# Attention and an expert layer on one core: the kv products of two heads as separate half-width matmuls, left-over tiles whole

## The chip, the cores and the metric

One core of a Trainium2 chip runs the program. The metric is the device time of one execution in microseconds. Before the change three runs took 923.88, 923.95 and 925.03 us; their median is 923.95 us. The engines named below are PE (matrix engine, with PEld for the loads of its stationary operand), DVE (vector), ACT (scalar), POOL and SP, whose queue issues most of the DMAs.

## The reference

```python
def _attn_ref(q, k, v):                    # each (8, 8, 576, 64): batch, head, row, column
    q_s = np.exp(q - np.max(q, axis=-1, keepdims=True))
    q_s = q_s / (np.sum(q_s, axis=-1, keepdims=True) + 1e-09)
    k_s = np.exp(k - np.max(k, axis=2, keepdims=True))
    k_s = k_s / (np.sum(k_s, axis=2, keepdims=True) + 1e-09)
    kv = np.einsum('bhsd,bhse->bhde', k_s, v)
    return np.einsum('bhsd,bhde->bhse', q_s, kv)

def _moe_ref(x, w_in, w_out, s, b):        # x (4608, 512), w_in (512, 2048), w_out (2048, 512)
    r = np.maximum(x @ w_in, 0.0)
    return (s * (r * r) + b) @ w_out
```

The attention's result, heads beside each other, is x. q is made a softmax along its 64 columns, k along its 576 rows; kv is a 64x64 matrix for each head. All arrays are f32.

## The kernel before

**Tiling.** The two heads 2u and 2u+1 form a unit u, two units a pair pr of four heads. A batch has two pairs, 16 in all. The 576 rows of a head are four tiles of 128 rows and a left-over of 64 (`NQ` 4, `LEFT` 64, `NT` 5). A unit's k tile is 128 partitions by five tiles by two heads by 64 columns.

**Expert layer.** For each block of 512 rows and each of 16 chunks of w_in and w_out, twelve h matmuls (line 524) make a 128x512 tile, ACT and DVE turn it into g, and twelve acc matmuls (line 597) add it to the output. h and acc use operands split in a high and a low part, so three products each. There are nine blocks: one for each batch, and one for the left-over rows of all.

**Batch 0** (lines 292 to 389) runs beside the loading and splitting of the weights (`conv_w`, lines 181 to 219). Its streams, `k_stream`, `kv_stream`, `q_stream`, the weight conversions and the steps of the expert layer, are put in one order for PE, DVE, ACT and SP by a planner (`Order`), which works with an estimated cost and a due time for each piece: `Op("PE", 2.6, ...)` is the kv group. `k_stream` transposes a unit's k tile by tile (line 300), takes the maximum and the exponential along the free axis and transposes back (lines 313 and 314). v lies head by head (`by_head`), 64 columns each.

**Later batches** go through `pair` (line 391 on), a generator that is advanced between the steps of the expert layer; a scheduler then fixes the order of each engine. There v lies by tile with both heads of a unit beside each other and a 129th column of ones (`v_tile`), which gives the sum of k's exponentials in the same matmul. The rows beyond the left-over are zeros in k, set by a memset after each exponential (line 425).

**The kv product**, in both places: for each unit and row tile one matmul with both heads' 128 k columns as the stationary operand and both heads' v as the moving one.

```python
nc.tensor.matmul(kv[:, i, :], kts[i][:, n].rearrange("p h d -> p (h d)"), vt[:, i, n, :], start=(n == 0), stop=(n == NT - 1))   # line 444
```

Of the 128x128 result only the two 64x64 blocks on the diagonal, head with its own head, are used (lines 341 and 453); the other two mix two heads and are dropped. In batch 0 the product and the transposes of the left-over tile take only its 64 rows (`m = P if n < NQ else LEFT`, lines 299 and 327). After the product come DVE's `z` and reciprocal, the scaling of four 64x64 blocks into `kvf`, its split, and the product with q (`xp`).

Of the kernel before, what the change touches and what calls it, by code (L numbers as in the profile page):

```python
# [8 lines left out]
F32 = mybir.dt.float32  # L9
# [3 lines left out]
AF = mybir.ActivationFunctionType  # L13
ALU = mybir.AluOpType
# [11 lines left out]
def attention_moe(ctx: ExitStack, tc: tile.TileContext, q, k, v, w_in, w_out, s, b, out):  # L26
    nc = tc.nc
    B, H, S, D = q.shape
    DM, FF = w_in.shape
    DO = w_out.shape[1]  # L30
    P = 128
    NP = H // 2
    NFC = FF // P
    NQ = 4
    LEFT = S - NQ * P
    NT = NQ + 1
# [17 lines left out]
    ps = ctx.enter_context(tc.tile_pool(name="ps", bufs=1, space=bass.MemoryType.PSUM))  # L54


    ident = const.tile([P, P], F32, name="ident")
    make_identity(nc, ident)

    kvfs = [const.tile([P, 2, 2, D], F32, name=f"kvf{i}") for i in range(2)]  # L60
    for t in kvfs:
# [4 lines left out]

    KQ, VW = 4 * NT * D, 2 * NT * (2 * D + 1)
    second = xpool.tile([P, 2 * NP * TB], F32, name="raw1", tag="x")  # L70
    raws = [
        (const.tile([P, KQ], F32, name="k0"), const.tile([P, KQ], F32, name="q0"), const.tile([P, VW], F32, name="v0")),
        (second[:, 0:KQ], second[:, KQ:2 * KQ], second[:, 2 * KQ:2 * KQ + VW]),
    ]

    def by_head(t):
        return t[:, 0:KQ].rearrange("p (h n d) -> p h n d", h=4, d=D)

    def by_tile(t):
        return t.rearrange("p (u n h d) -> p u n h d", u=2, h=2, d=D)  # L80

    def v_tile(t):
        return t.rearrange("p (u n e) -> p u n e", u=2, n=NT)

    for kt, qt, vt in raws:
        nc.gpsimd.memset(by_head(qt)[LEFT:P, :, NQ, :], 0.0)
    nc.gpsimd.memset(by_tile(raws[0][0])[LEFT:P, :, NQ], 0.0)

# [150 lines left out]
    def sources(pr):  # L241
        bb, hq = divmod(pr, NP // 2)
        h0 = 4 * hq

        def main(t, i, n):
            return t[bb, h0 + i:h0 + i + n, 0:NQ * P, :].rearrange("h (p n) d -> p h n d", n=NQ)

        def left(t, i, n):
            return t[bb, h0 + i:h0 + i + n, NQ * P:S, :].rearrange("h p d -> p h d")

        return main, left

    def load_k(pr, i):
        main, left = sources(pr)
        kt = by_tile(tiles[pr][0])
        for h in range(2):
            nc.sync.dma_start(kt[:, i, 0:NQ, h], main(k, 2 * i + h, 1)[:, 0])
        nc.sync.dma_start(kt[0:LEFT, i, NQ], left(k, 2 * i, 2))

    def load_heads(pr, which, eng):  # L260
        main, left = sources(pr)
        t = by_head(tiles[pr][which])
        eng.dma_start(t[:, :, 0:NQ, :], main((q, v)[which - 1], 0, 4))
        eng.dma_start(t[0:LEFT, :, NQ, :], left((q, v)[which - 1], 0, 4))

    def loads(pr):
        tiles[pr] = raws[0]
        main, left = sources(pr)
        for i in range(2):
            load_k(pr, i)  # L270
        load_heads(pr, 1, nc.sync)
        vt = v_tile(tiles[pr][2])
        if pr == NP:
            nc.gpsimd.memset(vt[LEFT:P, :, NQ, 0:2 * D], 0.0)
            nc.gpsimd.memset(vt[:, :, :, 2 * D:2 * D + 1], 1.0)
        for i in range(2):
            for h in range(2):
                nc.sync.dma_start(vt[:, i, 0:NQ, h * D:(h + 1) * D], main(v, 2 * i + h, 1)[:, 0])
            nc.sync.dma_start(vt[0:LEFT, i, NQ, 0:2 * D].rearrange("p (h d) -> p h d", h=2), left(v, 2 * i, 2))

    def bc(t, shape):
        return t.unsqueeze(3).to_broadcast(shape)

# [2 lines left out]
    def wide(u):  # L288

        return ("acc", 2) if u < NP else ("big", 1)  # L290

    def k_stream(u):
        pr, i = divmod(u, 2)
        due, (tag, bufs) = DUE[u], wide(u)
        yield Op("PE", 0.6, due, needs=[f"k{u} there"], take=[tag, "ke"])
        kt = by_tile(tiles[pr][0])
        kT = ps.tile([P, 2, 512], F32, name=f"kT_{u}", tag=tag, bufs=bufs).rearrange("p a b -> p (a b)")
        for n in range(NT):
            m = P if n < NQ else LEFT
            nc.tensor.transpose(kT[:, n * P:n * P + m], kt[0:m, i, n].rearrange("p h d -> p (h d)"), ident[0:m, 0:m])  # L300
        yield Op("DVE", 0.67, due)
        km = small.tile([P, 1], F32, name=f"km_{u}", tag="km")
        nc.vector.tensor_reduce(out=km, in_=kT[:, 0:S], axis=AX.X, op=ALU.max, negate=True)
        yield Op("ACT", 0.71, due, free=[tag])
        if pr not in zs:
            zs[pr] = small.tile([P, 2], F32, name=f"z_{pr}", tag="z")
        ke = work.tile([P, S], F32, name=f"ke_{u}", tag="qh")
        nc.scalar.activation(ke, kT[:, 0:S], AF.Exp, bias=km, accum_out=zs[pr][:, i:i + 1])

        yield Op("PE", 0.55, due, take=[tag], free=["ke"])  # L310
        kn = ps.tile([P, 2, 512], F32, name=f"kn_{u}", tag=tag, bufs=bufs).rearrange("p a b -> p (a b)")
        for n in range(NQ):
            nc.tensor.transpose(kn[:, n * P:(n + 1) * P], ke[:, n * P:(n + 1) * P], ident)
        nc.tensor.transpose(kn[0:LEFT, TB:TB + P], ke[:, TB:S], ident)
        yield Op("ACT", 0.63, due, free=[tag], gives=[f"k{u}"])
        nc.scalar.copy(kt[:, i, 0:NQ], kn[:, 0:TB].rearrange("p (n h d) -> p n h d", n=NQ, h=2))
        nc.scalar.copy(kt[0:LEFT, i, NQ], kn[0:LEFT, TB:TB + P].rearrange("p (h d) -> p h d", h=2))

    def kv_stream(pr):
        us = (2 * pr, 2 * pr + 1)  # L320
        due = DUE[us[1]]
        yield Op("PE", 2.6, due, needs=[f"k{u}" for u in us] + [f"v{pr} there"], take=["sm"], gives=[f"kv{pr}"])
        kt, vt = by_tile(tiles[pr][0]), by_head(tiles[pr][2])
        kv = ps.tile([P, 512], F32, name=f"kv_{pr}", tag="sm", bufs=1)[:, 0:4 * D].rearrange("p (u e) -> p u e", u=2)
        for i in range(2):
            for n in range(NT):
                m = P if n < NQ else LEFT
                nc.tensor.matmul(
                    kv[:, i].rearrange("p (h d) -> p h d", h=2), kt[0:m, i, n].rearrange("p h d -> p (h d)"),
                    vt[0:m, 2 * i:2 * i + 2, n, :], start=(n == 0), stop=(n == NT - 1)  # L330
                )
        yield Op("DVE", 0.15, due)
        z = zs.pop(pr)
        nc.vector.tensor_scalar(z, z, 1e-9, None, op0=ALU.add)
        zr = small.tile([P, 2], F32, name=f"zr_{pr}", tag="zr")
        nc.vector.reciprocal(zr, z)
        yield Op("ACT", 1.28, due, free=["sm"], gives=[f"kvf{pr}"])
        for i in range(2):
            for h in range(2):
                r = slice(h * D, (h + 1) * D)  # L340
                nc.scalar.activation(kvfs[pr % 2][r, i, h, :], kv[r, i, r], AF.Copy, scale=zr[r, i:i + 1])

    def q_stream(u):
        pr, i = divmod(u, 2)
# [46 lines left out]
    def pair(pr):  # L391
        us = (2 * pr, 2 * pr + 1)
        bb = us[0] // NP
        kt, qt, vt = tiles.pop(pr)
        kt, qt, vt = by_tile(kt), by_head(qt), v_tile(vt)
        kts, qts = [kt[:, i] for i in range(2)], [qt[:, 2 * i:2 * i + 2] for i in range(2)]

        def sm(n):
            return ps.tile([P, 512], F32, name=f"{n}_{pr}", tag="sm", bufs=1)
# [9 lines left out]
        kT = sm("kT")  # L409
# [19 lines left out]
        for i in range(2):  # L429
            u, qt = us[i], qts[i]  # L430
# [6 lines left out]
            qes.append(qe)  # L437
            yield

        EW = 2 * D + 1  # L440
        kv = sm("kv")[:, 0:2 * EW].rearrange("p (u e) -> p u e", u=2)
        for i in range(2):
            for n in range(NT):
                nc.tensor.matmul(kv[:, i, :], kts[i][:, n].rearrange("p h d -> p (h d)"), vt[:, i, n, :], start=(n == 0), stop=(n == NT - 1))  # L444
        z = small.tile([P, 2], F32, name=f"z_{pr}", tag="z")
        nc.vector.tensor_scalar(z, kv[:, :, 2 * D], 1e-9, None, op0=ALU.add)
        zr = small.tile([P, 2], F32, name=f"zr_{pr}", tag="zr")
        nc.vector.reciprocal(zr, z)
        kvf = kvfs[pr % 2]
        for i in range(2):  # L450
            for h in range(2):
                r = slice(h * D, (h + 1) * D)
                nc.vector.tensor_scalar(kvf[r, i, h, :], kv[r, i, r], zr[r, i:i + 1], None, op0=ALU.mult)
        kvhl = work.tile([P, 2, 2, 2 * D], F32R, name=f"kvhl_{pr}", tag="m2")
        split(kvf.rearrange("p u h d -> p u (h d)"), kvhl[:, 0], kvhl[:, 1], nc.scalar.copy, nc.gpsimd)
        yield
# [38 lines left out]
        for i in range(2):  # L495
            normalize(i)
            yield
            t = transpose(i)
# [183 lines left out]
    with tc.issue_after(fetched[-1].ins):  # L682
        loads(NP)
# [67 lines left out]
```

## Time and profile before

| what | value |
|---|---|
| median of the runs | 923.95 us |
| the profiled execution, whole | 925.23 us |
| its span, first to last instruction | 923.0 us |
| mean granted clock of PE | 0.996 |
| DVE busy from 50 to 60 us | 9.90 of 10 us |
| DVE busy from 346.6 to 445 us | 48.38 of 98.4 us |
| kv groups (line 328) in batch 0 | 4, of 20 records each |
| kv groups (line 444) later | 12, of 20 records each |
| records of line 444 on PE | 240, from 172.0 to 707.9 us |

An f32 matmul appears as two records of PE and two weight loads of PEld; an f32r matmul (h, acc) as one of each. A record's shape is written rows*columns of the stationary operand, then partitions x elements of the result. Matmuls are pipelined, so their durations overlap; how long a group holds the engine is read from the chain of work or from the distance of starts.

### The profile page before, as it was taken

The page shows a single profiled execution, that of the slowest core. Times are in us where ns is not written, and L with a number is a line of the kernel's source. Part 1 is how long each engine was busy: PE and PEld are TensorE (multiplying, and loading weights), DVE is VectorE, ACT ScalarE, POOL GpSimd, SP SyncE. Part 2 cuts the span into 40 slices and gives each one's busy share as a digit, 9 for nine tenths or more (in the row PEclk, how much of TensorE's full clock was granted, in tenths as well). Part 3 has the DMA queues.
Part 4 walks back from the last instruction along what each step waited for, and adds up shares of the span by engine and source line. Part 5 has one row for each costly group of instructions (what it writes and reads, how often), then busy time and mean ns, then how long its engine had stood idle before and what let it go on. Part 6 is the DMA issues. An engine that isn't in the chain of part 4 may idle for free.

```text
span 923.0 us, 10924 instructions
## 1 busy us (share of the span) xinstructions
PE 898.4 (97%) x4240; PEld 741.0 (80%) x4240; DVE 470.8 (51%) x731; ACT 366.8 (40%) x590; POOL 82.3 (9%) x101
## 2 busy tenths in 40 slices
PE   4799999999999999999999999999999999999997
PEld 3577778888888888888888888888888888888885
DVE  5999993545364636463455445453645332223222
ACT  4899874323332333243233333232333332222222
POOL 0000000202020201110021102020202020000000
PEclk9999999999999999999999999999999999999999
DMA  8891431303031201302130313030210110001001
GB/s 224 256 376 51 140 81 46 77 4 77 4 95 30 66 16 47 78 16 68 46 77 3 77 49 78 4 78 4 85 42 0 49 46 1 1 0 46 1 1 46
DMA packets 101731, 57.33 MB, mean 62 GB/s; under 512 B 78512, under 2 KB 96944, under 8 KB 101552
## 3 DMA queue, kind: packets, MB, share of 16 engines
q1 hardware_dynamic: 99760, 54.94, 21.2%
q10 hardware_dynamic: 1920, 1.70, 0.6%
q8 instruction: 33, 0.54, 0.3%
q14 instruction: 18, 0.15, 0.1%
HBM read 46.14 MB, written 10.49 MB: 61 GB/s over the span
## 4 chain that ended last, share of the span: by engine, by line
PE 87%; DMA 4%; DVE 4%; ACT 3%; issue 1%; ACTq 0%; SPq 0%; DVEq 0%
PE acc L597 40%; PE h L524 39%; PE kv L444 3%; PE xp L487 2%; DMA st<-in_moe_w_in_dram 2%; PE qT L470 1%; DMA v<-in_v_dram 1%; DMA st<-in_moe_w_out_dram 1%; DVE low L198 1%; DVE w L214 1%; DMA raw<-in_q_dram 0%; ACT low L192 0%; ACT w L212 0%; ACT st L195 0%; DVE x L389 0%
## 5 line engine op out<-in xcount | busy, mean ns | idle before, releaser
L524 PE MATMUL h<-x,w 128*128 128x512 f32 x1728 | 425.0, 393 | 1.3 <-ACT r L557 1.2
L524 PEld LDWEIGHTS h<-x,w 128*128 128x128 f32 x1728 | 321.7, 188 | 69.3 <-ACT r L557 3.5
L597 PE MATMUL acc<-w,gh 128*128 128x512 f32 x1152 | 345.8, 393 | 1.4 <-ACT o L609 1.4
L545 DVE SCALAR_TENSOR_TENSOR r<-r,sb 128x512 f32<-128x512 f32 x128 | 101.3, 791 | 299.3 <-ACT r L544 299.2
L597 PEld LDWEIGHTS acc<-w,gh 128*128 128x128 f32 x1152 | 214.1, 188 | 45.8 <-ACT o L609 2.1
L597 PE MATMUL acc<-w,gl 128*128 128x512 f32 x576 | 211.2, 393 | 0.7 <-DVE gl L537 0.6
L544 ACT ACTIVATE r<-h 128x512 f32<-128x512 f32 x128 | 76.5, 597 | 320.4 <-PE h L524 315.7
L537 DVE SCALAR_TENSOR_TENSOR gl<-r,sb,gh 128x512 fp32r<-128x512 f32 x132 | 102.8, 778 | 75.1 <-ACT gh L546 73.0
L597 PEld LDWEIGHTS acc<-w,gl 128*128 128x128 f32 x576 | 108.2, 188 | 26.1 <-DVE gl L537 2.4
L546 ACT ACTIVATE gh<-r,sb 128x512 fp32r<-128x512 f32 x128 | 92.7, 724 | 83.7 <-DVE r L545 83.1
L434 POOL TENSOR_TENSOR q<-q,qm 128x640 f32<-128x640 f32 x24 | 30.3, 1262 | 444.6 <-DVE qm L433 444.6
L464 POOL TENSOR_TENSOR qe<-qe,qr 128x640 f32<-128x640 f32 x24 | 30.3, 1262 | 48.7 <-DVE qr L463 44.5
L444 PE MATMUL kv<-v,k 128*128 128x129 f32 x240 | 28.8, 274 | 0.0
L444 PEld LDWEIGHTS kv<-v,k 128*128 128x128 f32 x240 | 28.2, 191 | 0.5
L436 ACT ACTIVATE qe<-q 128x640 f32<-128x640 f32 x24 | 17.6, 732 | 22.7 <-POOL q L434 22.7
L424 ACT ACTIVATE k<-k 128x640 f32<-128x640 f32 x24 | 17.6, 736 | 22.3 <-DVE k L419 22.3
L460 DVE TENSOR_REDUCE qs<-qe 128x10 f32<-128x640 f32 x24 | 19.6, 818 | 12.1 <-ACT qe L436 12.0
L95 DVE TENSOR_TENSOR x<-xp,x 128x512 fp32r<-128x512 f32 x24 | 16.6, 691 | 17.8 <-ACT x L94 17.6
L487 PE MATMUL xp<-qh,kvhl 128*128 128x256 f32 (+1 forms) x96 | 23.4, 297 | 0.0
L95 DVE TENSOR_TENSOR ql<-qT,qh 128x576 fp32r<-128x576 f32 x24 | 18.2, 756 | 7.7 <-ACT qh L94 7.6
L419 DVE TENSOR_TENSOR k<-k,mb 128x640 f32<-128x640 f32 x24 | 18.6, 815 | 6.1 <-PE mb L417 6.1
L94 ACT CAST qh<-qT 128x576 fp32r<-128x576 f32 x24 | 15.4, 640 | 14.1 <-PE qT L470 14.1
(97 smaller groups left out, 569.3 us busy)
## 6 DMA issues: line engine op xcount, KB each, us to landing
st<-in_moe_w_in_dram SPq DMA_DIRECT2D x16, 512.0 KB, 9.5
st<-in_moe_w_out_dram SPq DMA_DIRECT2D x16, 512.0 KB, 9.8
out_dram<-o SPq DMA_DIRECT2D x16, 512.0 KB, 2.7
k<-in_k_dram SPq DMA_DIRECT2D x60, 128.0 KB, 3.1
q<-in_q_dram SPq DMA_DIRECT2D x14, 512.0 KB, 4.4
v<-in_v_dram SPq DMA_DIRECT2D x48, 128.0 KB, 3.0
v<-in_v_dram SPq DMA_DIRECT2D x2, 512.0 KB, 4.1
xleft<-xleft SPq DMA_DIRECT2D x16, 64.0 KB, 1.7
```

The costliest lines, as they stand in the source:

```text
L95: return eng_l.tensor_tensor(out=l, in0=src, in1=h.bitcast(F32), op=ALU.subtract)
L434: nc.gpsimd.tensor_tensor(out=qt, in0=qt, in1=bc(qm, [P, 2, NT, D]), op=ALU.subtract)
L444: nc.tensor.matmul(kv[:, i, :], kts[i][:, n].rearrange("p h d -> p (h d)"), vt[:, i, n, :], start=(n == 0), stop=(n == NT - 1))
L460: nc.vector.tensor_reduce(out=qs, in_=qe, axis=AX.X, op=ALU.add)
L464: nc.gpsimd.tensor_tensor(out=qe, in0=qe, in1=bc(qr, [P, NT, 2, D]), op=ALU.mult)
L487: nc.tensor.matmul(t[:, 0:src.stop - src.start], lhs, rhs[:, src], start=(j == 0), stop=(j == len(terms) - 1))
L524: nc.tensor.matmul(hp_, w[:, j, c, :], x[:, c, :], start=(c == 0 and i == 0), stop=(c == NP - 1 and i == 2))
L537: gls.append(nc.vector.scalar_tensor_tensor(out=gl, in0=r, scalar=b_col, in1=gh.bitcast(F32), op0=ALU.add, op1=ALU.subtract))
L544: nc.scalar.activation(r, hp_, AF.Relu)
L545: nc.vector.scalar_tensor_tensor(out=r, in0=r, scalar=s_col, in1=r, op0=ALU.mult, op1=ALU.mult)
L546: nc.scalar.activation(gh, r, AF.Identity, bias=b_col)
L597: last = nc.tensor.matmul(a, g[:, js], w_, start=(f == 0 and i == 0), stop=(f == NFC - 1 and i == 2)).ins
```

## The change

Each kv matmul of a unit becomes two, one for each head. A head's 64 k columns are the stationary operand, and its own 64 columns of v the moving one; the two heads of a unit write to the lower and the upper 64 partitions of the same PSUM columns. The products that mix two heads are no longer computed. Both places call the new function `heads`. To give each head a column of ones, v lies head by head with 65 columns in all batches (`v_tile`). The four heads' left-over rows of v come by one DMA, not two.

In batch 0 the left-over tile is used whole, so its other 64 rows in k and v of both buffers are set to zero at the start; and the planner's estimate of the kv group goes from 2.6 to 1.4.

```diff
-    KQ, VW = 4 * NT * D, 2 * NT * (2 * D + 1)
+    KQ, VW = 4 * NT * D, 4 * NT * (D + 1)
...
     def v_tile(t):
-        return t.rearrange("p (u n e) -> p u n e", u=2, n=NT)
+        return t.rearrange("p (h n e) -> p h n e", h=4, n=NT)

     for kt, qt, vt in raws:
-        nc.gpsimd.memset(by_head(qt)[LEFT:P, :, NQ, :], 0.0)
-    nc.gpsimd.memset(by_tile(raws[0][0])[LEFT:P, :, NQ], 0.0)
+        nc.gpsimd.memset(by_tile(kt)[LEFT:P, :, NQ], 0.0)
+        for t in (qt, vt):
+            nc.gpsimd.memset(by_head(t)[LEFT:P, :, NQ, :], 0.0)
...
         if pr == NP:
-            nc.gpsimd.memset(vt[LEFT:P, :, NQ, 0:2 * D], 0.0)
-            nc.gpsimd.memset(vt[:, :, :, 2 * D:2 * D + 1], 1.0)
-        for i in range(2):
-            for h in range(2):
-                nc.sync.dma_start(vt[:, i, 0:NQ, h * D:(h + 1) * D], main(v, 2 * i + h, 1)[:, 0])
-            nc.sync.dma_start(vt[0:LEFT, i, NQ, 0:2 * D].rearrange("p (h d) -> p h d", h=2), left(v, 2 * i, 2))
+            nc.gpsimd.memset(vt[LEFT:P, :, NQ, 0:D], 0.0)
+            nc.gpsimd.memset(vt[:, :, :, D:D + 1], 1.0)
+        for h in range(4):
+            nc.sync.dma_start(vt[:, h, 0:NQ, 0:D], main(v, h, 1)[:, 0])
+        nc.sync.dma_start(vt[0:LEFT, :, NQ, 0:D], left(v, 0, 4))
...
+    def heads(kv, kt, vt):
+
+        for i in range(2):
+            for n in range(NT):
+                for h in range(2):
+                    nc.tensor.matmul(
+                        kv[h * D:(h + 1) * D, i], kt[:, i, n, h], vt[:, 2 * i + h, n], start=(n == 0), stop=(n == NT - 1)
+                    )
...
         for n in range(NT):
-            m = P if n < NQ else LEFT
-            nc.tensor.transpose(kT[:, n * P:n * P + m], kt[0:m, i, n].rearrange("p h d -> p (h d)"), ident[0:m, 0:m])
+            nc.tensor.transpose(kT[:, n * P:(n + 1) * P], kt[:, i, n].rearrange("p h d -> p (h d)"), ident)
...
-        yield Op("PE", 2.6, due, needs=[f"k{u}" for u in us] + [f"v{pr} there"], take=["sm"], gives=[f"kv{pr}"])
+        yield Op("PE", 1.4, due, needs=[f"k{u}" for u in us] + [f"v{pr} there"], take=["sm"], gives=[f"kv{pr}"])
         kt, vt = by_tile(tiles[pr][0]), by_head(tiles[pr][2])
-        kv = ps.tile([P, 512], F32, name=f"kv_{pr}", tag="sm", bufs=1)[:, 0:4 * D].rearrange("p (u e) -> p u e", u=2)
-        for i in range(2):
-            for n in range(NT):
-                m = P if n < NQ else LEFT
-                nc.tensor.matmul(
-                    kv[:, i].rearrange("p (h d) -> p h d", h=2), kt[0:m, i, n].rearrange("p h d -> p (h d)"),
-                    vt[0:m, 2 * i:2 * i + 2, n, :], start=(n == 0), stop=(n == NT - 1)
-                )
+        kv = ps.tile([P, 512], F32, name=f"kv_{pr}", tag="sm", bufs=1)[:, 0:2 * D].rearrange("p (u d) -> p u d", u=2)
+        heads(kv, kt, vt)
...
-                nc.scalar.activation(kvfs[pr % 2][r, i, h, :], kv[r, i, r], AF.Copy, scale=zr[r, i:i + 1])
+                nc.scalar.activation(kvfs[pr % 2][r, i, h, :], kv[r, i], AF.Copy, scale=zr[r, i:i + 1])
...
-        EW = 2 * D + 1
-        kv = sm("kv")[:, 0:2 * EW].rearrange("p (u e) -> p u e", u=2)
-        for i in range(2):
-            for n in range(NT):
-                nc.tensor.matmul(kv[:, i, :], kts[i][:, n].rearrange("p h d -> p (h d)"), vt[:, i, n, :], start=(n == 0), stop=(n == NT - 1))
+        kv = sm("kv")[:, 0:2 * (D + 1)].rearrange("p (u e) -> p u e", u=2)
+        heads(kv, kt, vt)
...
-                nc.vector.tensor_scalar(kvf[r, i, h, :], kv[r, i, r], zr[r, i:i + 1], None, op0=ALU.mult)
+                nc.vector.tensor_scalar(kvf[r, i, h, :], kv[r, i, 0:D], zr[r, i:i + 1], None, op0=ALU.mult)
```

How the order of the instructions changes is shown at three places. The first is PE early in batch 0, at the first kv group; kT, kn and kv are the results of the transposes and the product, k, raw and v the loaded tiles. Before:

```order
L300 MATMUL kT_200<-ident,raw_88 128x128 x4
L300 MATMUL kT_200<-ident,raw_88 128x64
L328 MATMUL kv_215<-v_91,k_89 128x128 x10
L313 MATMUL kn_242<-ident,ke_228 128x128 x4
L314 MATMUL kn_242<-ident,ke_228 64x128
L300 MATMUL kT_256<-ident,raw_88 128x128 x4
L300 MATMUL kT_256<-ident,raw_88 128x64
L380 MATMUL xp_276<-qf_186,kvf_83 128x256
```

After:

```order
L308 MATMUL kT_203<-ident,raw_88 128x128 x5
L289 MATMUL kv_218<-v_91,k_89 64x64 x20
L321 MATMUL kn_251<-ident,ke_241 128x128 x4
L322 MATMUL kn_251<-ident,ke_241 64x128
L308 MATMUL kT_266<-ident,raw_88 128x128 x5
L382 MATMUL xp_283<-qf_189,kvf_83 128x256
```

The sequence is the same; the short fifth transpose is now like the other four, and ten products have become twenty.

The second place is PE at the first kv group of the later batches, between the expert layer's acc and h matmuls. Before:

```order
L597 MATMUL acc_2_1399<-w_446,gl_1424 128x512
L444 MATMUL kv_1471<-v_91,k_89 128x129 [waits DMAHW0_49,DMAHW5_49,DVE_49,DMAHW6_49,PE_49,DMAHW7_49,Activation_49,Pool_49]
L444 MATMUL kv_1471<-v_91,k_89 128x129 x3
L444 MATMUL kv_1471<-v_91,k_89 128x129 [waits DMAHW7_49,DMAHW1_49,Pool_49]
L444 MATMUL kv_1471<-v_91,k_89 128x129 [waits DMAHW2_49,DMAHW1_49,DMAHW3_49,DMAHW0_49,Activation_49]
L444 MATMUL kv_1471<-v_91,k_89 128x129 x3
L444 MATMUL kv_1471<-v_91,k_89 128x129 [waits DMAHW4_49,DMAHW2_49,Pool_49]
L524 MATMUL h_1511<-x_857,w_541 128x512 [waits Activation_49]
```

After:

```order
L596 MATMUL acc_2_1441<-w_471,gl_1466 128x512
L289 MATMUL kv_1513<-v_91,k_89 64x65 [waits DVE_49,PE_49,DMAHW5_49,Activation_49,Pool_49]
L289 MATMUL kv_1513<-v_91,k_89 64x65 [waits DMAHW6_49]
L289 MATMUL kv_1513<-v_91,k_89 64x65 x6
L289 MATMUL kv_1513<-v_91,k_89 64x65 [waits DMAHW7_49,DMAHW1_49,Pool_49]
L289 MATMUL kv_1513<-v_91,k_89 64x65
L289 MATMUL kv_1513<-v_91,k_89 64x65 [waits DMAHW7_49,DMAHW0_49,Activation_49]
L289 MATMUL kv_1513<-v_91,k_89 64x65 [waits DMAHW0_49]
L289 MATMUL kv_1513<-v_91,k_89 64x65 x6
L289 MATMUL kv_1513<-v_91,k_89 64x65 [waits DMAHW2_49,Pool_49]
L289 MATMUL kv_1513<-v_91,k_89 64x65
L523 MATMUL h_1563<-x_883,w_557 128x512 [waits Activation_49]
```

The group stands in the same surroundings, and waits for the same loads and engines, spread over more matmuls.

The third place is DVE early in batch 0, around the reciprocal of the first pair's sums z; qm and km are maxima, low and w parts of the weight conversion. Before:

```order
L352 TENSOR_REDUCE qm_236<-raw_88 128x10
L352 TENSOR_REDUCE qm_240<-raw_88 128x10
L334 TENSOR_SCALAR z_133<-z_133 128x2
L336 RECIPROCAL zr_252<-z_133 128x2
L354 TENSOR_TENSOR raw_88<-raw_88,qm_236 128x640
L303 TENSOR_REDUCE km_267<-kT_256 128x1
L354 TENSOR_TENSOR raw_88<-raw_88,qm_240 128x640
L214 TENSOR_TENSOR w_233<-low_0_166,w_233 128x512
```

After:

```order
L336 TENSOR_SCALAR z_136<-z_136 128x2
L338 RECIPROCAL zr_258<-z_136 128x2
L354 TENSOR_REDUCE qm_260<-raw_88 128x10
L354 TENSOR_REDUCE qm_272<-raw_88 128x10
L356 TENSOR_TENSOR raw_88<-raw_88,qm_260 128x640
L311 TENSOR_REDUCE km_280<-kT_266 128x1
L356 TENSOR_TENSOR raw_88<-raw_88,qm_272 128x640
L362 TENSOR_REDUCE qs_299<-qe_286 128x10
```

The reciprocal goes ahead of the two maxima of q, and the weight conversion's row moves further back.

More of the change, by code (lines that the diff above doesn't have):

```diff
@@ L438, in pair @@
             yield
-        EW = 2 * D + 1
-        kv = sm("kv")[:, 0:2 * EW].rearrange("p (u e) -> p u e", u=2)
-        for i in range(2):
-            for n in range(NT):
-                nc.tensor.matmul(kv[:, i, :], kts[i][:, n].rearrange("p h d -> p (h d)"), vt[:, i, n, :], start=(n == 0), stop=(n == NT - 1))
+        kv = sm("kv")[:, 0:2 * (D + 1)].rearrange("p (u e) -> p u e", u=2)
+        heads(kv, kt, vt)
         z = small.tile([P, 2], F32, name=f"z_{pr}", tag="z")
-        nc.vector.tensor_scalar(z, kv[:, :, 2 * D], 1e-9, None, op0=ALU.add)
+        nc.vector.tensor_scalar(z, kv[:, :, D], 1e-9, None, op0=ALU.add)
         zr = small.tile([P, 2], F32, name=f"zr_{pr}", tag="zr")
```

## The prediction

> **What bounds the kernel now.** I read the busy shares and the slices of the page first, then the chain of work that ended last, then the busy times by stage, then the kv groups themselves.
>
> ```profile
> span 923.0 us, 10924 instructions
> PE 898.4 (97%) x4240; PEld 741.0 (80%) x4240; DVE 470.8 (51%) x731; ACT 366.8 (40%) x590; POOL 82.3 (9%) x101
> ...
> PEclk9999999999999999999999999999999999999999
> ...
> PE 87%; DMA 4%; DVE 4%; ACT 3%; issue 1%; ACTq 0%; SPq 0%; DVEq 0%
> ...
> by line: PE acc L597 45.7%; PE h L524 45.2%; PE kv L444 3.5%; PE xp L487 2.5%; PE qT L470 1.7%; PE kT L411 0.3%; PE mb L417 0.3%; ACT o L609 0.2%; DVE o L609 0.1%; issue 0.0%; DVEq L609 0.0%
> ```
>
> The last of these lines is the chain asked for from 150 us to the end. There it runs on the matrix engine (PE) alone: nothing else has more than 0.2% of these 773 us, and 3.5% of them, 27 us, are the kv products of line 444. The clock is full throughout. So after 150 us a microsecond taken from PE is a microsecond off the kernel, until another engine is late; the vector engine (DVE) is busy only half of that time:
>
> ```profile
> core 0: us, PE busy (x) PEld busy (x) DVE busy (x) ACT busy (x) POOL busy (x), PEclk, DMA share, GB/s
> 80.00:90.00 10.00, 9.96 (x51) 7.63 (x50) 9.79 (x14) 9.21 (x16) 0.00 (x0) 1.00 0.11 32
> 90.00:100.00 10.00, 10.00 (x51) 8.13 (x51) 9.80 (x14) 9.15 (x14) 0.00 (x0) 1.00 0.55 141
> 100.00:110.00 10.00, 9.65 (x41) 6.76 (x39) 9.93 (x16) 9.13 (x15) 0.00 (x0) 1.00 0.69 223
> 110.00:120.00 10.00, 9.92 (x52) 7.99 (x53) 9.97 (x13) 8.93 (x16) 0.00 (x0) 1.00 0.01 2
> ...
> 150.00:248.30 98.30, 98.30 (x478) 82.47 (x477) 48.60 (x82) 34.10 (x57) 12.38 (x14) 1.00 0.19 49
> ```
>
> Batch 0 and the weights, up to 150 us, are another case: PE and DVE are both full, and a saving on PE alone is partly stopped by DVE.
>
> **The later batches, where the main term lies.** One kv group after 150 us, in the chain, and the form of its instructions:
>
> ```profile
> 170.98 1.36 PE acc L597 x6
> 172.34 2.23 PE kv L444 x20
> ...
> L444 PE MATMUL kv<-v,k 128*128 128x129 f32 x240 | 28.8, 274 | 0.0
> L444 PEld LDWEIGHTS kv<-v,k 128*128 128x128 f32 x240 | 28.2, 191 | 0.5
> ```
>
> An f32 matmul is two records, each a weight load and a pass; ten matmuls make 20 records, 2.23 us, so 0.1115 us a record. Loads of 191 ns and passes of 274 ns overlap, for one behind the other they would need far more. Twelve groups give 26.8 us, the 27 us of the chain.
>
> The change makes 20 matmuls, 40 records, of each group: 64 weight columns and 65 moving columns in place of 128 and 129. Two questions decide: what a half-size record takes, and whether the records of the two heads, which write different halves of the output's partitions, run beside each other.
>
> For the size, by proportion a record takes 0.1115 x 65/129 = 0.056 us. What 64 columns are worth elsewhere:
>
> ```profile
> L380 PE MATMUL xp<-qf,kvf 128*128 128x320 f32 x16 | 5.9, 453 | 0.0
> ...
> L380 PE MATMUL xp<-qf,kvf 128*128 128x256 f32 x16 | 5.3, 410 | 3.9 <-ACT qf L373 2.5 <-ACT kvf L341 0.7 <-DVE x L389 0.6
> ```
>
> 64 moving columns in f32 make 43 ns there, so at worst a record falls to 0.1115 - 0.043 = 0.069 us. With the heads side by side a group takes 20 x 0.056 = 1.12 to 20 x 0.069 = 1.38 us; one behind the other 2.24 to 2.76.
>
> The ends of a group have a price too if the array must empty when the width changes. In the first stage there is one such row with half the columns, a transpose between whole ones:
>
> ```profile
> 22.36 0.11 PEld L314 LDWEIGHTS kn<-ident,ke 128*64 128x64 f32 x1
> 22.46 0.47 PEld L300 LDWEIGHTS kT<-ident,raw 128*128 128x128 f32 x4
> 23.10 0.13 PEld L300 LDWEIGHTS kT<-ident,raw 64*128 64x128 f32 x1 [0.17 <-issue]
> ```
>
> The 64-column load starts 0.10 us ahead of the next whole one, with no hole, while the load with 64 rows waits 0.17 us for nothing named. Half the rows costs a hole, half the columns does not, so I put the ends at nothing, at most 0.2 us each. The Trainium skill ("TensorEngine Tiling (Array Packing)", Key Properties) says that changing the tiling mode, not just the tile, drains the engine; the hole before the 64-row load agrees, the 64-column row does not. By that rule each group would have two drains, and the saving below would be smaller by up to 12 x 0.4 = 4.8 us.
>
> That the heads run side by side no row of before shows, since each matmul there takes the whole array. The bounds are 1.12 and 2.76 us. I take 1.35, near the 1.38 of the dearer record: each matmul's own two records still follow one another, but the second of one head and the first of the other use different columns. Saved: 12 x (2.23 - 1.35) = **10.6 us**.
>
> What covers the rest here: each pair's v comes in by five DMAs and no longer six, from the sync queue, well ahead; the reciprocal and the scaling on DVE read the same 64x64 blocks; the column of ones is set once, for all later pairs. All of that lies beside PE. No wait is new: kv waits for the same loads and the same exponentials. What would be late next is the exponential's memset on POOL, and its queue is 12.4 us busy out of 98.
>
> **Batch 0.** Here the change also takes away the 64-row products and transposes, which stand between whole ones:
>
> ```profile
> 77.28 0.66 PE kn L313 x4
> ...
> 79.45 0.64 PE kT L300 x5
> 80.09 0.90 PE acc L597 x3
> ...
> 86.03 0.70 PE acc L597 x3
> ...
> 87.53 1.39 PE acc L597 x6
> 88.92 2.81 PE kv L328 x20
> 91.73 1.60 PE acc L597 x6
> ...
> 95.73 0.04 ACT x L386
> ...
> 130.08 0.69 DVE x L389
> ```
>
> A kv group takes 2.81 us, and the six acc matmuls behind it 1.60 and not 1.39: 3.02 us against 2.23 for whole tiles, so 0.8 us for four changes of height. With the halves it is 3.02 - 1.35 = 1.67 us, four times 6.7. A kT group makes the next three matmuls 0.90 and not 0.70 us: 0.2, eight times 1.6. That is 8.3 us of PE. How much shows? Between 77 and 96 us the chain runs on PE, with one kv and one kT in it: 1.67 + 0.2 = 1.9. From there to 130 us it goes through DVE and ACT, whose work doesn't change, and DVE was over 9.6 of 10 us busy. I take **1.9 us**. At best the later relief adds up too, some 5 us; at worst the order hurts: the kv estimate falls from 2.6 to 1.4 and the planner rearranges weight conversions against q work on DVE, whose longest single rows are 1.2 us. Two or three of those put ahead of something needed make +3. The three added memsets on POOL lie in the first microseconds, while k is still coming in:
>
> ```profile
> 2.50 0.31 POOL L87 MEMSET k<- 64x256 f32 x1
> ...
> L300 PE MATMUL kT<-ident,k 128*128 128x128 f32 x24 | 5.0, 347 | 8.0 <-DMA k<-in_k_dram 8.0
> ```
>
> Three more at 0.31 us end near 3.8 us; the first transpose waits for its DMA until about 8. Without that cover they would cost 0.9 us.
>
> **The sum.** 10.6 + 1.9 = 12.5 us. The profiled execution took 925.23 us (its span of 923.0 and 2.2 around it), 1.3 above the median of the runs, 923.95. 925.23 - 12.5 = 912.7, and 1.3 lower on the runs' scale: 911.4, said as **911.5**.
>
> **The rivals.**
> *The heads run one behind the other.* For it: nothing in before has two matmuls in different columns, and the loads could have one path, in which case 40 half loads take as long as 20 whole ones. Against: the half-column row passes with no hole, and the outputs share no partition. A group then takes 2.24 to 2.76 us: 0 to +6.4 us, with batch 0 still 0.8 x 4 less on PE, of which perhaps 1.5 shows: 922.5 to 929, most likely near the lower end, since both parts of a record scale with columns. So the change would do only the lesser thing that it says.
>
> *Slower: each change of head exposes the load.* If the next head's weights can't come in while the other head's pass runs, as with the 64-row rows above, each of 20 changes in a group is a hole. Cheapest, a half load of 0.056 us not covered: +1.1 us a group, 3.35, twelve times +13.4, so 935 after the 1.9 of batch 0. Dearest, the 0.2 us of a change of height (0.8 over four): +4 us a group, +48, so 972. It decides as soon as a change costs over some 0.008 us more than the passes one behind the other (1.9 / 240). Against it: in line 444 each load runs under the pass before it. The Trainium skill ("TensorE: Matmul & The Clock Gate", Part 3, The mechanism) says that a weight load overlaps with matmuls in flight only where the row group differs, or goes into the background buffer; here both heads use all rows, so by its first half loads and passes would alternate, 40 x 0.112 = 4.5 us a group, 951. The trace of before has loads under passes of the same rows (20 loads of 191 ns in 2.23 us), so it bears out only the second half.
>
> **How the numbers follow.** Side by side 0.64, one behind the other 0.27, exposed loads 0.09. The likeliest case alone reaches from 12 x (2.23 - 1.12) + 5 = 18.3 us saved, 905.5, to a group of 1.7 us (drains at both ends) with +3 in batch 0, 3.4 us saved, 920.5. The whole range also takes in most of the second case: **905 to 925**; above lie the slower rival and the dear end of the second, together 0.16, below 0.03. About 0.2%, 1.85 us, is what a measurement of this kernel can tell from no change. Faster: 0.62 of the first case and a third of the second, 0.71; same: 0.15; slower: 0.14.
>
> **What would show it.** In the profile after: a kv group in the chain after 150 us of 1.1 to 1.7 us with 40 records (right), 2.2 or more (second case), 3 or more with idle time ahead of the loads (third). The batch period falls from 98.3 us by about 1.8. The loads at the ends of a group show no hole as that of the 64-row load. In batch 0 no 64-row form is left, and 150 us becomes 146 to 149. I am wrong if the two heads' passes start as far apart as two records of one head, or if batch 0 ends later than before.

## The result, and the profile after

| | before | after |
|---|---|---|
| median of the runs | 924.49 us (923.88 to 926.74, 4 runs) | 909.70 us (909.13 to 912.15, 4 runs) |
| ratio after to before | | 0.9838, 95% interval 0.9825 to 0.9851 |
| the profiled execution, whole | 925.23 us | 909.13 us |
| its span | 923.0 us | 907.4 us |

911.5 was forecast. The medians lie 14.8 us apart, the profiled executions 16.1 (their spans 15.6: the last output behind the chain took 0.5 us longer). Where the 16.1 went is read at two places, the first and the last of the twelve later kv groups. The page of after, and its chain from 150 us on:

```profile
span 907.4 us, 11600 instructions
PE 881.9 (97%) x4560; PEld 723.4 (80%) x4560; DVE 470.8 (52%) x731; ACT 366.0 (40%) x590; POOL 82.7 (9%) x104
...
by line: PE acc L596 45.4%; PE h L523 44.8%; PE xp L486 2.5%; PE kv L289 2.0%; PE qT L469 1.7%; PE mb L419 0.3%; PE kT L413 0.3%; ACT o L608 0.2%; DVE o L608 0.1%; issue 0.0%; DVEq L608 0.0%
```

DVE, ACT and POOL do the work they did, but for three more memsets on POOL. PE is still the whole chain after 150 us; its share for kv fell from 3.5% to 2.0%. The first and the last later group in the chain of after (start, length, what):

```profile
162.04 2.72 PE acc L596 x12
164.75 1.32 PE kv L289 x40
166.07 2.93 PE h L523 x12
...
690.72 1.32 PE kv L289 x40
692.04 2.05 PE acc L596 x8
```

and the last one in the chain of before:

```profile
706.09 2.23 PE kv L444 x20
708.32 1.84 PE acc L597 x8
```

The first later group starts at 164.75 instead of 172.34 us: 7.6 us were gained up to there. The last starts at 690.72 instead of 706.09, 15.4 us earlier, so the eleven groups from the one to the other gained 7.8 us: **0.71 us each**, 8.5 for twelve. In these two executions the gain has two halves of nearly equal size, 7.6 in batch 0 and 8.5 in the later batches. A profile holds twelve later groups but only one batch 0; by the medians its part is 14.8 - 8.5 = 6.3.

The two executions also differ in the clock of batch 0. The figure behind the five busy times is the granted clock, first in before, then in after:

```profile
30.00:42.00 12.00, 9.46 (x43) 6.85 (x42) 11.73 (x18) 11.48 (x18) 0.00 (x0) 0.87 0.71 200
```

```profile
30.00:42.00 12.00, 8.60 (x39) 6.39 (x40) 11.86 (x17) 10.52 (x17) 0.00 (x0) 1.00 1.03 311
```

A clock of 0.87 over 12 us is, by an estimate from this row, at most 1.6 us of PE's work. So up to that much of the 7.6 may come from the clock and not from the change.

Inside a later group the chain shows 0.91 us less (1.32 for 2.23), and then the twelve h matmuls behind it take 2.93 and not the 2.72 to 2.76 of others: 0.2 comes back at the end. The loads and passes around the group, first in before, then in after:

```profile
171.95 0.39 PE L597 MATMUL acc<-w,gl 128*128 128x512 f32 x1
171.96 2.43 PEld L444 LDWEIGHTS kv<-v,k 128*128 128x128 f32 x20
172.18 2.39 PE L444 MATMUL kv<-v,k 128*128 128x129 f32 x20
```

```profile
164.14 0.19 PEld L596 LDWEIGHTS acc<-w,gl 128*128 128x128 f32 x1
164.68 1.25 PEld L289 LDWEIGHTS kv<-v,k 128*64 128x64 f32 x40 [0.35 <-issue]
166.00 0.76 PEld L523 LDWEIGHTS h<-x,w 128*128 128x128 f32 x4
```

```profile
164.37 0.39 PE L596 MATMUL acc<-w,gl 128*128 128x512 f32 x1
164.69 0.45 PE L289 MATMUL kv<-v,k 128*64 128x65 f32 x8
```

Three things are to be seen. The group's first load stands idle for 0.35 us after the one before it, waiting for nothing that the profile names; in before it started at 171.96, under the pass ahead of it, which started at 171.95. Eight passes are under way within a quarter of a microsecond: in the trace the passes of a later group start in pairs, 2 to 9 ns apart within a pair and some 58 ns from pair to pair, 107 from the first pair to the second; 20 pairs start within 1.17 us. And the load of the next h matmul comes after the group's last pass, not under it.

### The profile page after: what moved, and what is told of

It is laid out like the page before. It is cut to its first block, busy times and chain, and to the rows that moved or that the text cites. A ratio compares the mean times of both kernels' runs of the same rounds, so it can differ in the third digit from the quotient of the medians.

```text
span 907.4 us, 11600 instructions
## 1 busy us (share of the span) xinstructions
PE 881.9 (97%) x4560; PEld 723.4 (80%) x4560; DVE 470.8 (52%) x731; ACT 366.0 (40%) x590; POOL 82.7 (9%) x104
## 4 chain that ended last, share of the span: by engine, by line
PE 85%; DVE 10%; ACT 2%; issue 2%; DMA 1%; ACTq 0%; DVEq 0%
PE acc L596 40%; PE h L523 39%; PE xp L486 2%; DVE low L199 2%; PE kv L289 2%; DVE w L215 2%; PE qT L469 1%; DVE low L208 1%; DVE st L205 1%; DVE st L203 1%; DMA k<-in_k_dram 1%; DVE qm L354 1%; DMA q<-in_q_dram 1%; DVE gl L566 0%; DVE q L356 0%
## 5 line engine op out<-in xcount | busy, mean ns | idle before, releaser
L596 PE MATMUL acc<-w,gh 128*128 128x512 f32 x1152 | 340.2, 392 | 1.4 <-ACT o L608 1.4
L596 PE MATMUL acc<-w,gl 128*128 128x512 f32 x576 | 208.3, 394 | 0.8 <-DVE gl L566 0.8
L95 ACT CAST qh<-qT 128x576 fp32r<-128x576 f32 x24 | 15.4, 640 | 19.9 <-PE qT L469 19.9
L289 PEld LDWEIGHTS kv<-v,k 128*64 128x64 f32 x600 | 19.6, 143 | 4.2 <-issue 2.8
L289 PE MATMUL kv<-v,k 128*64 128x65 f32 (+1 forms) x600 | 21.7, 229 | 0.0
```

The source lines that it names most:

```text
L289: nc.tensor.matmul(kv[h * D:(h + 1) * D, i], kt[:, i, n, h], vt[:, 2 * i + h, n], start=(n == 0), stop=(n == NT - 1))
L596: last = nc.tensor.matmul(a, g[:, js], w_, start=(f == 0 and i == 0), stop=(f == NFC - 1 and i == 2)).ins
```

## The experiments

Times are medians against before in the same series of runs. Where batches are told apart, it is by the start of the first later kv group in the chain (172.34 us in before, 164.75 in after) and of the last.

### One size: the width of v's tile

```diff
-    KQ, VW = 4 * NT * D, 2 * NT * (2 * D + 1)
+    KQ, VW = 4 * NT * D, 4 * NT * (D + 1)
...
-        return t.rearrange("p (u n e) -> p u n e", u=2, n=NT)
+        return t[:, 0:2 * NT * (2 * D + 1)].rearrange("p (u n e) -> p u n e", u=2, n=NT)
```

> The kernel before with one size changed: v's tile is 1300 numbers wide instead of 1290, all products as before. In before, ACT's fourth DMA issue (line 264, left-over rows of v) starts only at 9.07 us, 7 us after the third, and the first exponential follows at 11.14; in after the issue starts at 2.65 and the exponential at 9.76. Theory A: the tile's width alone takes that wait away (the dependency between the two v loads is a matter of the layout), and part of the 7.6 us that after gains by the end of batch 0 is this: exponential at about 9.8 us, the kernel 1.4 to 4.5 us faster, 920 to 923. Theory B: the gain of batch 0 is all matrix engine work that fell away: exponential perhaps earlier, but the kernel within 1 us of before, 924.

Measured: 923.09 us against 925.32, ratio 0.998 (0.9968 to 0.9992), 2.2 us faster and just above A's 920 to 923. ACT's first instructions in before:

```profile
1.98 0.61 ACTq L263 DMA_DIRECT2D v<-in_v_dram  x1
9.07 0.62 ACTq L264 DMA_DIRECT2D v<-in_v_dram  x1
9.85 1.28 ACT L357 ACT_TABLE_LOAD   x1 [9.85 <-DMA k<-in_k_dram]
11.14 0.74 ACT L357 ACTIVATE qe<-q 128x640 f32<-128x640 f32 x1
```

and in this kernel:

```profile
2.01 0.61 ACTq L263 DMA_DIRECT2D v<-in_v_dram  x1
2.65 0.63 ACTq L264 DMA_DIRECT2D v<-in_v_dram  x1
8.79 1.28 ACT L357 ACT_TABLE_LOAD   x1 [8.79 <-DVE q L354]
10.08 0.74 ACT L357 ACTIVATE qe<-q 128x640 f32<-128x640 f32 x1
```

In before the issue of v's left-over rows starts at 9.07 us and not at 2.65. It waits for the load ahead of it, which was issued at 1.98 and took 7.00 us to land, and it holds the table load and the first exponential behind it on ACT's queue. Both loads stand in the chain that ended last in before:

```profile
1.98 7.00 DMA v<-in_v_dram
...
9.07 5.50 DMA v<-in_v_dram
```

In the chain of this kernel neither stands. So ten more numbers of width remove the wait, and the medians give 2.2 us for them: theory A. The way from the one to the other isn't shown in full. The first exponential is only 1.06 us earlier. And the one profile of this kernel, the slowest of its ten runs (926.44, of 921.48 to 926.44), has its first later group at 173.46 us, 1.1 later than in before; its granted clock was 0.94 from 30 to 60 us, as in before.

### Only the later groups

```diff
-        yield Op("PE", 1.4, due, needs=[f"k{u}" for u in us] + [f"v{pr} there"], take=["sm"], gives=[f"kv{pr}"])
+        yield Op("PE", 2.6, due, needs=[f"k{u}" for u in us] + [f"v{pr} there"], take=["sm"], gives=[f"kv{pr}"])
...
-        heads(kv, kt, vt)
+        for i in range(2):
+            for n in range(NT):
+                m = P if n < NQ else LEFT
+                nc.tensor.matmul(
+                    kv[:, i].rearrange("p (h d) -> p h d", h=2), kt[0:m, i, n].rearrange("p h d -> p (h d)"),
+                    vt[0:m, 2 * i:2 * i + 2, n, :], start=(n == 0), stop=(n == NT - 1)
+                )
```

and the transposes, the memsets and the kv tile of batch 0 as in before; `pair` stays as in after.

> The changed kernel with batch 0 put back (full-width products, 64-row left-over, planner cost 2.6); half-width products only in the twelve later groups, v's tile 1300 wide. Later groups should each take 0.71 us less than in before, 8.5 in all, whatever explains batch 0. Theory A (the width of v's tile gives about half of batch 0's 7.6 us): 911.5 to 913.5. Theory B (batch 0's gain is its own products): 916.

Measured: 913.66 us against 925.32, ratio 0.9882 (0.9862 to 0.9902), just above the range of A and below B. Its chain has

```profile
169.88 1.32 PE kv L288 x40
...
695.85 1.32 PE kv L288 x40
```

2.5 us gained up to the first later group, and 525.97 us from there to the last, as in after (690.72 - 164.75 = 525.97; before 533.75). So the later groups' gain stands by itself. All of batch 0's own change, products, left-over and order, is worth the other 5.1 us in the profiles and 4.0 in the medians (913.66 against 909.70).

### Batch 0: products and order apart

The estimate alone decides what order the planner makes: the kernel with an estimate of 2.6 has the order of the one above, whatever the products (in the traces the first 170 rows of DVE and of ACT stand in the same order in the two kernels of each estimate). Two kernels complete a square of products and order:

```diff
-        yield Op("PE", 1.4, due, needs=[f"k{u}" for u in us] + [f"v{pr} there"], take=["sm"], gives=[f"kv{pr}"])
+        yield Op("PE", 2.6, due, needs=[f"k{u}" for u in us] + [f"v{pr} there"], take=["sm"], gives=[f"kv{pr}"])
```

> The changed kernel with only the planner's estimate of the kv group back at 2.6. Theory A (the order that the estimate makes matters little, since the vector engine is full in batch 0 either way): within 1.5 us of after, 908.5 to 911.5. Theory B (the new order is what gained in batch 0): 2 to 5 us slower than after, 912 to 915.

and the kernel of the last section with its estimate at 1.4:

> Batch 0 with its old products (full width, 64-row left-over), but in the order that the planner makes from an estimate of 1.4, the very order of after on every engine; v's tile 1300 wide, later groups halved. It completes a square: old products at 2.6 gained 2.4 us by the end of batch 0, new products at 2.6 gained 3.1, new products at 1.4 gained 7.6. Theory A (the order alone makes the difference): about 7 by the end of batch 0, 909.5 to 911.5. Theory B (the order pays only with the shorter products, which it counts on): 2 to 4 by the end of batch 0, 912.5 to 915. Theory C (the order is worse with products twice as long as it counts on): below 2, 915 or more.

Measured: 913.23 us (ratio 0.9869, 0.9855 to 0.9884) and 914.59 us (0.989, 0.9867 to 0.9912; its runs spread from 912.64 to 916.57). The first later group in their chains, first with the new products at 2.6, then with the old ones at 1.4:

```profile
169.23 1.32 PE kv L289 x40
```

```profile
168.44 1.32 PE kv L288 x40
```

| batch 0, v's tile wide | estimate 2.6 | estimate 1.4 |
|---|---|---|
| old products | 913.66 us; group at 169.88 | 914.59 us; group at 168.44 |
| new products | 913.23 us; group at 169.23 | 909.70 us; group at 164.75 |

Against the corner of old products at 2.6, the short products alone gain 0.4 us in the medians (0.7 in the profile), and the new order alone loses 0.9 (1.4 gained in the profile); both together gain 4.0 (5.1). The single steps can't be told from nothing: each place of a group comes from one profile, and wide_v and the old products at 2.6, whose batch 0 has the same work, lie 3.6 us apart there (173.46 and 169.88). The clock differs too: from 30 to 60 us it was 0.94 in the profile of the new products at 2.6 and 1.00 in the other three. That the new products at 1.4 stand apart from the rest is shown by the medians, and by the kernels with 1.5 and 1.6 below. This is B of both expectations: the order pays where the products are as short as it assumes.

Three more estimates, all else as in after:

> The changed kernel with an estimate of 1.6 instead of 1.4, that is on the other side of the 1.5 that a group takes. Theory A (an estimate near the real time makes a better order): within 1 us of after, 909 to 911. Theory B (each estimate draws another order, and 1.4 was a lucky one): anywhere from 909 to 914, with the difference all made before 150 us.

> The changed kernel with an estimate of 2.0, half way between 1.4 and 2.6. Theory A (nearer to the truth is better): between the two, 910.5 to 912.5. Theory B (each estimate draws another order): anywhere from 908 to 914, not in order with the estimates.

> The changed kernel with the estimate at 1.5, the time that a group took. Estimates of 1.4, 1.6, 2.0 and 2.6 gave 909.7, 909.5, 911.2 and 913.2. Theory A (the nearer to the truth the better, and flat near it): 908.5 to 910.5. Theory B (each estimate draws another order): 909 to 914, with the difference made before 150 us.

| estimate | median, us | range of 4 runs | first later group at |
|---|---|---|---|
| 1.4 (after) | 909.70 | 909.13 to 912.15 | 164.75 |
| 1.5 | 908.89 | 908.23 to 909.54 | 164.06 |
| 1.6 | 909.50 | 909.27 to 909.70 | 165.44 |
| 2.0 | 911.18 | 910.87 to 912.08 | 166.75 |
| 2.6 | 913.23 | 912.28 to 913.63 | 169.23 |

The times fall as the estimate nears the 1.5 us that a later group costs PE, and are flat from 1.6 to 1.4: A. The orders are alike where the estimates are: of the first 170 rows of DVE, 33 stand at another place at 1.5 than at 1.4, 31 at 1.6, 50 at 2.0 and 107 at 2.6. No estimate below 1.4 was tried, so whether one that is too short would cost time again is not shown. 1.5 is the best version here (ratio to before 0.9828, 0.9811 to 0.9844), though not to be told from after. Which of the rearranged rows on DVE makes the difference was not tried.

### One head after the other

```diff
-            for n in range(NT):
-                for h in range(2):
+            for h in range(2):
+                for n in range(NT):
```

> The changed kernel with the loops over heads and tiles exchanged: five products of the lower half, then five of the upper half, per unit. Theory A (two halves run side by side only where neighbours in the program differ in columns): 40 records 0.056 us apart, a later group 2.2 us from its first to its last start in place of 1.17, twelve times +1.07 and some of it in batch 0: 922 to 927. Theory B (each half of the columns has a queue of its own, and five records deep doesn't matter): no change, 910. Theory C (no overlap at all, a record is just cheap): no change, 910, with the starts evenly spaced in both.

Measured: 917.73 us, ratio 0.9918 (0.9903 to 0.9933): none of the three, between A and B. The first and last later group:

```profile
165.02 1.95 PE kv L289 x40
...
698.00 1.95 PE kv L289 x40
```

1.95 us in the chain and not 1.32; from first to last 532.98 us, 7.0 more than in after. In the trace the starts behind the opening are 56 to 61 ns apart, until the first pair; a group has nine pairs, of 2 to 7 ns, and its starts span 1.79 us, not the 2.2 of A. So the upper half does start beside the lower while products of that are left, though it stands behind all five of them in the program, and C falls. Of the 7.8 us that the eleven groups gained, 0.8 is left (533.75 - 532.98): nearly all of the gain needs neighbours in the program that use different halves. Batch 0 ends as in after (165.02), though the clock was 0.94 from 30 to 60 us here too; so such a dip cost little in this profile.

### What a change of width costs

```diff
-    def heads(kv, kt, vt):
+    def heads(kv, kt, vt, between=None):
...
         for i in range(2):
+            if i == 1 and between is not None:
+                nc.tensor.transpose(between, ident, ident)
             for n in range(NT):
...
-        heads(kv, kt, vt)
+        heads(kv, kt, vt, kvp[:, 256:256 + P])
```

`kvp` is the whole PSUM tile of which kv takes the first columns.

> The changed kernel with one full-width transpose of the identity, into unused columns of the same PSUM tile, between the two units of each of the twelve later groups; it computes nothing that is used. In after a later group costs 1.52 us though its starts span only 1.17: the load of the first half-width record waits for the last full-width one, and the other way round at the end. Theory A (each change between full and half width empties the array, 0.18 us): two changes more, and 0.11 for the transpose, 0.46 a group, 5.5 in all: 914 to 916. Theory B (the ends cost what they do because of the waits on semaphores at the group's first and last matmul): 0.11 a group, 1.3 in all: 910.5 to 911.5.

Measured: 914.96 us, ratio 0.9896 (0.9877 to 0.9916): A. A later group in its chain:

```profile
165.75 0.73 PE kv L291 x20
166.48 0.26 PE kv L288
166.74 0.73 PE kv L291 x20
167.47 2.99 PE h L526 x12
```

1.72 us and 2.99 behind it, against 1.32 and 2.93: 0.46 more, of which 0.11 is the transpose. The last two kernels put one half-width instruction into before's full-width groups, so that no upper half and no pair of halves is there:

```diff
         for i in range(2):
+            if i == 1:
+                nc.tensor.matmul(kvp[0:D, 384:384 + D], ident[:, 0:D], ident[:, 0:D], start=True, stop=True)
             for n in range(NT):
```

> The kernel before, with one matmul of 64 stationary columns (identity by identity, lower half of the columns, into unused PSUM columns, not used) between the two units of each of the twelve later groups, which stay full width. Read from the gap between the starts of the last record of the first unit and the first of the second, 0.11 us in before. Theory A (any half-width product empties the array, at its start and at its end): a gap of about 0.11 + 2 x 0.06 + 2 x 0.18 = 0.6 us. Theory B (only the pair of halves, or the upper half, empties it): 0.2 to 0.25 us.

and with `nc.tensor.transpose(kvp[0:D, 384:512], ident[:, 0:D], ident)` in its place:

> The same with a transpose of 64 columns, the form that stood without a hole between full-width transposes in before (line 314). Theory A (a transpose in the lower half does not empty the array, whatever its neighbours): a gap of about 0.2 us, 0.11 more than in before. Theory B (it does so between products): about 0.55 us.

One run each gave 930.75 and 928.38 us, with before at 924.81; of the second, 1.3 us are made before the first later group (173.65 against 172.34), where nothing was changed. A later group with the half-width product, then one with the half-width transpose, in their chains:

```profile
172.29 1.12 PE kv L447 x10
173.40 0.26 PE kv L445 x2
173.66 1.31 PE kv L447 x10
174.97 2.76 PE h L527 x12
```

```profile
173.65 1.12 PE kv L447 x10
174.77 0.11 PE kv L445
174.88 1.12 PE kv L447 x10
175.99 2.78 PE h L527 x12
```

The product makes the group 2.69 us long, 0.46 more than 2.23. By an estimate its own two records are 0.11 of this (2 x 0.055, half of a full one each), so each change costs 0.17. The gap between the starts of the neighbouring full records was 0.46 us in all twelve groups, between B's 0.25 and A's 0.6 and nearer to A; the next two starts are 0.21 apart and not 0.11, which is the rest of the price. The transpose adds 0.12 us, its own time, with a gap of 0.22: A. So a half-width product costs a hole before it and behind it, and a half-width transpose does not. The two differ in more than their kind: the product is two records with 64 moving columns, the transpose one with 128. Which of these makes the hole was not tried.

## Why the prediction was right

**What bounds it.** Right for the later batches: after 150 us each microsecond off PE came off the kernel, 0.71 us a group (0.67 to 0.74 in each of the eleven intervals), and no other engine's share of the chain grew. A batch of two groups fell by 1.42 us, from 98.25 to 96.83, where the prediction's sign was 1.8. That the clock is full throughout was misread: it was 0.87 from 30 to 42 us in before.

**Size of a record, and side by side.** Right, and cheaper than taken: 0.058 us from pair to pair, next to the lower bound of 0.056 (proportion) and not the 0.069 of the f32 rows by which 1.35 was chosen. All 20 pairs of a group run side by side, also the two first records.

**The ends of a group.** Wrong: put at nothing, measured at 0.17 each. With them a group costs PE 1.52 us (2.23 less 0.71), not 1.35. The row that I leaned on, the 64-column load without a hole, was a transpose, and narrow_tr shows that such a row says nothing on products. The bound of 0.2 a change had covered the price, and the term of 10.6 us became 8.5. The Trainium skill ("TensorEngine Tiling (Array Packing)", Key Properties) says that a change of the tiling mode drains the engine: the products' holes of 0.17 us agree, and at the transposes no hole shows.

**Batch 0.** Mis-sized: 1.9 us, 5 at best, measured 6.3 by the medians and 7.6 in the profile, so the sign of 146 to 149 us in place of 150 was passed too. Two steps failed. One I hadn't seen: v's tile became ten numbers wider, and a wait of 6.4 us on ACT's queue went; that is some 2 us by the medians. The other was the order: I let it only hurt. The matrix engine's relief by itself gave 0.4 us in the medians and 0.7 in the profile, not to be told from nothing, and not the 1.9 that I took; with an estimate that fits the products the planner's order turned it into 4.0 (5.1 in the profile). That a full DVE is what held the relief back was argued and not tried.

**The sum** was right to 1.8 us, and part of that is luck: 2.1 us too much in the later groups stand against 4.4 too little in batch 0 (5.7 in the profile), and the two errors come from different steps. The rest is the start: 911.5 was taken from 923.95, the median of three runs of before, and a fourth run moved it to 924.49. Between the medians 14.8 us were gained, between the profiled executions 16.1, and not 12.5.

**The rivals.** One head behind the other: not in the changed kernel, and with the loops exchanged only in part. Exposed loads at each change of head: refuted, 2 to 9 ns between the heads of a pair; only the second pair, 107 ns behind the first, stands off. The Trainium skill ("TensorE: Matmul & The Clock Gate", Part 3, The mechanism) says that loads overlap with matmuls in flight only where the row group differs, or go into the background buffer. By its first half the prediction had estimated 4.5 us a group; the starts of a group span 1.17 with both heads on the same rows, so that half doesn't hold here.

## What to carry to other kernels

Here 20 f32 products of 64 stationary columns that write the two halves of the partitions in turn took 1.52 us, where ten of 128 columns took 2.23. Each passage between half and full width cost 0.17 us of that, so such products should stand in groups; a single one among full-width products cost 0.46. Where a planner sets the order, its estimate is part of the change: measure the new time and put it in. One profile can't price a stage that varies from run to run by some microseconds, as batch 0 does; the medians of several runs are needed. And compare the first waits of each queue before and after, since a change of a tile's size can remove or make one.

## What the runs showed that I had not expected

- The two heads' first records start together, though in the program each product's two records stand one behind the other: a product in the other half of the columns does not wait for the rest of the one before it. With one head after the other this reaches some way past neighbouring products, nine pairs a group in place of 20; how far, and what limits it, stays open.
- A transpose of 64 columns between full-width products cost 0.12 us, a product of 64 columns 0.46.
- Ten f32 of width in a tile decided whether one DMA's issue waited 6.4 us for another. Why the narrower tile made them depend on each other was not tried.
